# The mixer's head of an S4-plus-MLP block in another order, with its generation phase

## The chip, the cores and the metric
The kernel runs on one core of one Trainium2 chip. The metric is device time in microseconds (us) for one call; the time before is the median of three runs. Profiles come from one execution of each kernel, with a time of its own.

## The reference
One block of width 512 over 2048 tokens, in fp32. A condition vector gives six modulation vectors; the first three belong to a state-space layer (a convolution with a generated kernel, by a Fourier transform), the last three to a mixer (a shift of channels along the tokens, then an MLP of width 1376).

```python
mod = (silu(c) @ w_mod).reshape(1, 6, 1, 512)
sa, ca, ga, sb, cb, gb = (mod[:, i] for i in range(6))
h = layernorm(x) * (1 + ca) + sa
x = x + ga * ssm(h)          # K = Re(sum_n C*dB*exp(dt*A*l)); y = irfft(rfft(h)*rfft(K)) + h*Dskip
h = layernorm(x) * (1 + cb) + sb
g = gelu(layernorm(h) @ w1)  # four quarters of the channels shifted by +1, -1, +2, -2 tokens
x1 = h + shifted(g) @ w2
x = x + gb * (x1 + gelu(layernorm(x1) @ w3) @ w4)
```

## The kernel before
The order of the work is written out by hand; each engine runs its own instructions in program order and waits at each for what it needs. There are five stages.

1. **Preparation** (to about 42 us): angles and weights of the state-space kernel on VectorE and ScalarE.
2. **Generation** (to about 222 us): 32 steps k. `turns(k, 0)` and `turns(k, 1)` build angles on TensorE, and ScalarE takes sine (`sn`) and cosine (`cs`) of them, two steps ahead. `products(k)` on VectorE multiplies them with magnitudes into `e0` and `e1`: the small factor `m1` (line 478), two products with the sine for `e0` (482), one for `e1` (483), one with the cosine for `e0` (484) and one for `e1` (485). `burst(k)` on TensorE sums `e0` and `e1` into the kernel `KX`. Every fourth step `exps` makes the next magnitudes (function Exp, so ScalarE loads another table and then the sine's again). `fill(n)` issues n matmuls whose result nobody reads. The Fourier transform of the input (`u_stats`, `u_norm`, `u_dft`) is spread over these steps.
3. **Spectrum** (to about 354 us): 16 steps multiply spectra; `back` writes `z` through the GpSimd queue to a scratch `ZT` in DRAM.
4. **The mixer's head** (to about 442 us). `load_inv(jh, g)` reads `ZT` back in four blocks for the second half of the channels (jh = 1); `inverse(jh, g)` transforms block g back: token tiles 4g to 4g+3, in two halves i of two tiles each. VectorE adds the result to the residual `X2` (line 692). A mixer group g is two token tiles: statistics of `X2` (`first_stats`), the modulated row `h` (`modulate`: lines 725 and 726), its statistics, on GpSimd the inverse root and the shift (`rs`, `nm`), on ScalarE the normalization (`mix_norm`), on TensorE the transposes `pT`, then the high part `nh` (ScalarE) and the low part `nl` (VectorE, line 751), and two halves of the product with `w1` (`mix_half`: 24 matmuls each, Gelu to `go`, and `mix_out`, which writes `go` to the scratch `GD`). The head works groups 7, 0, 1, 2, 3. The shift is done by reading `GD` with an offset (`chan_load`), so `chan_load(0)` needs the outputs of groups 7, 0 and 1. The weights `w3` and `w4` are loaded (`load_w`) and split in two parts (`split_w`) in between. `chan_w2(0)` multiplies with `w2`, then statistics, `chan_norm(0)`, and the transposes for `chan(0)`.
5. **Channel MLP** (from about 442 us to the end): eight groups `chan(g)`, with the mixer groups 4 to 6 woven into the first of them.

`mix_out` issues from GpSimd's queue; the loads issue from SP's queue. `gop` has two buffers for `go`, `hv` one for `win`.

Of the kernel before, what the change touches and what calls it, by code (L numbers as in the profile page):

```python
# [15 lines left out]
TWO_PI = 6.283185  # L16
# [93 lines left out]
def body(ctx, tc, A):  # L110
# [171 lines left out]
    with tc.manual_schedule():  # L282
# [59 lines left out]
        wr, wi, t0, t1 = tmp("wr"), tmp("wi"), tmp("t0"), tmp("t1")  # L342
        V.tensor_mul(wr, cr, br)
# [26 lines left out]
        V.tensor_mul(mn, mn, mx)  # L370
        at, at0, wn = tmp("at"), tmp("at0"), tmp("wn")
        act(at0, mn, AF.Arctan)
        act(wn, at0, AF.Sin, scale=-1.0, bias=hpi)
        mp = [mod_parts(n) for n in range(2)]
# [11 lines left out]
        V.tensor_scalar(at, at0, INV2PI, None, op0=OP.mult)  # L386
# [13 lines left out]
        V.reciprocal(wn, wn)  # L400
        V.tensor_mul(wn, wn, mc)
        V.tensor_tensor(as4(wn), as4(wn), by(dt), op=OP.mult)
        wps = psu.tile([128, 512], F32, name="pu")
        for i in range(4):
            s = slice(i * 128, (i + 1) * 128)
            T.transpose(wps[:, s], wn[:, s], ident)
        act(WN, wps)
        mod_parts(2)()
        mod_sum(2)()
        load_u(1)  # L410
        V.tensor_mul(mods[1], mods[1], mods[2])
        V.tensor_mul(mods[0], mods[0], mods[2])
# [40 lines left out]
    def turns(k, cos):  # L453
# [10 lines left out]
        o = wk.tile([128, 2, 512], F32, name="cs" if cos else "sn", bufs=3)  # L464
        act(o.rearrange("p a b -> p (a b)"), x, AF.Sin, scale=-TWO_PI, bias=hpi if cos else 0.0)
        return o

    trig = {}

    def products(k):  # L470
        t, u = divmod(k, 4)
        sn, cs = trig.pop(k)
        mg, pt = PE[t][0][u], PE[t][1][:, u]
        e0 = wk.tile([128, 2, 2, 512], F32, name="e0")
        e1 = wk.tile([128, 2, 16, 32], F32, name="e1")
        f2 = lambda z: z.rearrange("p a b -> p (a b)")
        m1 = wk1.tile([128, 16, 32], F32, name="m1")
        V.tensor_mul(m1.rearrange("p d (x y) -> p d x y", x=4),
                     pt[:, :, None, :8].to_broadcast([128, 16, 4, 8]),
                     pt[:, :, 8:12, None].to_broadcast([128, 16, 4, 8]))  # L480
        for a in range(2):
            V.scalar_tensor_tensor(e0[:, 1, a], sn[:, 0], 1.0 - 2.0 * a, mg[:, a], op0=OP.mult, op1=OP.mult)  # L482
        V.tensor_mul(f2(e1[:, 1]), sn[:, 1], f2(m1))
        V.tensor_mul(e0[:, 0], cs[:, 0:1].to_broadcast([128, 2, 512]), mg)  # L484
        V.tensor_mul(f2(e1[:, 0]), cs[:, 1], f2(m1))  # L485
        return e0, e1
# [44 lines left out]
    with tc.manual_schedule():  # L531
        for k in range(2):
            trig[k] = turns(k, 0), turns(k, 1)
        weigh(0)
        for k in range(33):
            now, later = later, []
            if 1 in KP:
                fill(3)
            for f in now:
                f()  # L540
            if k + 2 < 32:
                trig[k + 2] = turns(k + 2, 0), turns(k + 2, 1)
            if k < 32:
# [5 lines left out]
                if fresh:  # L549
                    KP[1] = psk.tile([128, 8, 64], F32, name="kp")  # L550
                    fill(3)
                    for u in range(2, 5):
                        exps(k // 4 + 1, u, u + 1)
                        fill(2)
                if k % 4 == 3 and k < 28:
                    weigh(k // 4 + 1)
            for f in side[k]:
                f()
# [120 lines left out]

    def inverse(jh, g):  # L680
        zz = zis.pop((jh, g))
        for i in range(2):
            p = psy.tile([128, 2, 256], F32, name="py")
            for e in range(2):
                for h in range(2):
                    b = g * 4 + i * 2 + e
                    cc = 15 - b if h == 0 else b
                    T.matmul(p[h * 64:h * 64 + 64, e], FI[:, cc, h], zz[h][:, cc % 4],
                             start=True, stop=True, skip_group_check=True)
            b = g * 4 + i * 2  # L690
            x = X2[:, b:b + 2, jh * 256:jh * 256 + 256]
            V.tensor_add(x, p, x)
# [30 lines left out]

    def modulate(o, b):
        V.scalar_tensor_tensor(o, X2[:, b], mv1[:, b, 0:1], mods[4], op0=OP.subtract, op1=OP.mult)  # L725
        V.scalar_tensor_tensor(o, o, rs1[:, b:b + 1], mods[3], op0=OP.mult, op1=OP.add)  # L726
# [3 lines left out]

    def first_rstd(g):
        rstd(rs1[:, 2 * g:2 * g + 2], mv1[:, 2 * g:2 * g + 2, 1])

    def first_stats(g):
        for b in (2 * g, 2 * g + 1):
            first_stat(b)
        first_rstd(g)
# [18 lines left out]
    def mix_mod_half(g, i):  # L756
        if i == 0:
            mh[g] = (cm.tile([128, 2, 512], F32, name="h2"), cm.tile([128, 2, 2], F32, name="mv"),
                     cm.tile([128, 2], F32, name="rs"), cm.tile([128, 2], F32, name="nm"))
        h, mv, r, nm = mh[g]  # L760
        modulate(h[:, i], 2 * g + i)
        stats(mv[:, i], h[:, i])
        if i == 1:
            rstd(r, mv[:, :, 1])
            P.tensor_tensor(nm, mv[:, :, 0], m_one[:, :2], op=OP.mult)
            P.tensor_tensor(nm, nm, r, op=OP.mult)
            mh[g] = h, r, nm

    def mix_mod(g):
        mix_mod_half(g, 0)  # L770
        mix_mod_half(g, 1)

    def mix_norm(g):
        h, r, nm = mh[g]
# [17 lines left out]
    def mix_out(g, hf, go):  # L792
        P.dma_start(dram(GD, (2 + 2 * g) * 128 + hf * 256 * 2560, [[2560, 128], [128 * 2560, 2], [1, 256]]), go)
# [15 lines left out]
        P.dma_start(dram(GD, (18 if g == 0 else 0) * 128 + hf * 256 * 2560, [[2560, 128], [128 * 2560, 2], [1, 256]]), pd)  # L809
# [102 lines left out]
    def chan(g, hl):  # L912
# [11 lines left out]
        def mod(i):  # L924
            if t is not None:
                mix_mod_half(t, i)
                if i == 1:
# [6 lines left out]
        def half(hf):  # L934
            if t is not None:
                mix_half(t, st["hl"], hf)
                if t < 6:
                    first_stat(2 * t + 2 + hf)
                    if hf == 1:
                        first_rstd(t + 1)  # L940
# [77 lines left out]
    with tc.manual_schedule():  # L1018
# [52 lines left out]
        psw = ctx.enter_context(tp("psw", 2, space=PSUM))  # L1071
        load_inv(1, 3)
# [3 lines left out]
        inverse(1, 3)  # L1076
        load_inv(1, 2)
        first_stats(7)
        mix_mod(7)
        mix_norm(7)  # L1080
        inverse(1, 0)
        hl = parts_of(transposed(mh.pop(7)[0]))
        first_stats(0)
        mix_mod(0)
        first_stats(1)
        mix_norm(0)
        inverse(1, 1)
        mix_mod(1)
        first_stats(2)
        mix_half(7, hl, 0)  # L1090
        nt = transposed(mh.pop(0)[0])
        p1 = mix_w(hl, 1)
        hl = parts_of(nt)
        mix_norm(1)
        go = gop.tile([128, 2, 256], F32, name="go")
        act(go, p1, AF.Gelu_apprx_tanh)
        mix_out(7, 1, go)
        inverse(1, 2)
# [8 lines left out]
        mix_mod(2)  # L1107
        mix_half(0, hl, 0)
        nt = transposed(mh.pop(1)[0])
        p1 = mix_w(hl, 1)  # L1110
        hl = parts_of(nt)
        mix_norm(2)
        go = gop.tile([128, 2, 256], F32, name="go")
        act(go, p1, AF.Gelu_apprx_tanh)
        mix_out(0, 1, go)
        first_stats(3)
        mix_half(1, hl, 0)
        nt = transposed(mh.pop(2)[0])
        p1 = mix_w(hl, 1)
        hl = parts_of(nt)  # L1120
        go = gop.tile([128, 2, 256], F32, name="go")
        act(go, p1, AF.Gelu_apprx_tanh)
# [43 lines left out]
```

## Time and profile before

| | |
|---|---|
| median of 3 runs | 769.93 us (769.35 to 771.09) |
| the profiled execution | 766.72 us, its span 764.9 us |
| TensorE matmul busy | 693.8 us (91%) |
| VectorE busy | 512.9 us (67%) |
| ScalarE busy | 332.8 us (44%) |
| GpSimd busy | 98.1 us (13%) |
| mean granted TensorE clock | 0.952 |

The median lies 3.2 us above the profiled execution. The shares are means over stages that have different limits, so the stages are read one by one: in a stretch where an engine is busy all the time, its work is the limit, and where all of them idle, a chain of waits is. A row of the timeline gives the start, the duration, the engine, the line and the operation; the brackets give the idle time before it and what ended that.

### The profile page before, as it was taken

What the parts mean: (1) busy time and instruction counts of PE and PEld (TensorE: products, weight loads), DVE (VectorE), ACT (ScalarE), POOL (GpSimd) and SP (SyncE); (2) the same over time, 40 slices, a digit from 0 to 9 for tenths busy, and PEclk for the clock granted to TensorE, in tenths of its full rate; (3) what the DMA queues carried; (4) which work ended last, traced back from release to release, by engine and by line L of the source; (5) the groups of instructions that cost most, each with busy time, mean ns of one, the idle gap of its engine ahead of it and who ended that gap; (6) DMA issues with size and microseconds to landing.
All of it is one profiled execution on the core that took longest, in us unless ns stands there. A gap on an engine that the chain in (4) does not pass through costs nothing. (4 is left out here: it accounts for less than half of the span.)

```text
span 764.9 us, 17371 instructions
## 1 busy us (share of the span) xinstructions
PE 693.8 (91%) x7340; PEld 540.2 (71%) x7340; DVE 512.9 (67%) x883; ACT 332.8 (44%) x540; POOL 98.1 (13%) x194
## 2 busy tenths in 40 slices
PE   2799999999989999995578799999999999999993
PEld 1356666665569656662368698999999998998992
DVE  8999999999873576774695696655565545353611
ACT  3678888887843445533133453312223121212120
POOL 1011121110000001000145110112021010100101
PEclk9999999999995899998789799999999999999997
DMA  9523282645259994884316701111110111101001
GB/s 299 164 66 83 71 235 77 168 131 149 57 130 258 243 334 152 274 251 167 137 40 230 246 29 28 29 38 46 32 52 15 42 29 28 28 28 28 9 20 27
DMA packets 51301, 85.51 MB, mean 112 GB/s; under 512 B 5300, under 2 KB 37944, under 8 KB 49560
## 3 DMA queue, kind: packets, MB, share of 16 engines
q1 hardware_dynamic: 44808, 57.92, 27.3%
q0 software_dynamic: 6416, 26.48, 10.5%
q8 instruction: 58, 0.95, 0.5%
q14 instruction: 19, 0.16, 0.1%
HBM read 58.17 MB, written 31.85 MB: 118 GB/s over the span
## 5 line engine op out<-in xcount | busy, mean ns | idle before, releaser
L118 ACT ACTIVATE gh<-pm 128x512 fp32r<-128x512 f32 (+1 forms) x48 | 26.9, 561 | 202.1 <-PE pm L784 202.1
L781 PE MATMUL pm<-nh,w3h 128*128 128x256 f32 (+1 forms) x352 | 87.9, 283 | 0.4 <-ACT nh L118 0.4
L782 PE MATMUL pm<-nh,w3l 128*128 128x256 f32 (+1 forms) x352 | 87.4, 281 | 0.0
L885 DVE TENSOR_TENSOR gl<-gf,gh 128x512 fp32r<-128x512 f32 (+1 forms) x48 | 30.9, 643 | 72.0 <-ACT gf L118 72.0
L894 PE MATMUL pa<-w4h,gh 128*128 128x512 f32 (+1 forms) x176 | 69.5, 395 | 0.0
L895 PE MATMUL pa<-w4l,gh 128*128 128x512 f32 (+1 forms) x176 | 68.9, 391 | 0.0
L781 PEld LDWEIGHTS pm<-nh,w3h 128*128 128x128 f32 (+1 forms) x352 | 65.4, 186 | 2.0 <-ACT nh L118 0.6
L782 PEld LDWEIGHTS pm<-nh,w3l 128*128 128x128 f32 (+1 forms) x352 | 65.6, 186 | 1.7
L784 PE MATMUL pm<-nl,w3h 128*128 128x256 f32 (+1 forms) x352 | 56.1, 282 | 0.0
L784 PEld LDWEIGHTS pm<-nl,w3h 128*128 128x128 f32 (+1 forms) x352 | 47.8, 186 | 0.1
L900 PE MATMUL pa<-w4h,gl 128*128 128x512 f32 (+1 forms) x176 | 47.8, 390 | 0.0
L462 PE MATMUL xx<-MG,ON 64*128 64x512 f32 x160 | 47.4, 391 | 0.0
L463 PE MATMUL xx<-MG,ON 64*128 64x512 f32 x160 | 47.4, 391 | 0.0
L482 DVE SCALAR_TENSOR_TENSOR e<-sn,p 128x512 f32<-128x512 f32 x64 | 41.2, 685 | 4.7 <-ACT sn L118 4.7
L841 DVE TENSOR_TENSOR h<-h,ph 128x512 f32<-128x512 f32 x16 | 11.0, 688 | 45.9 <-PE ph L840 45.9
L502 PEld LDWEIGHTS kp<-e,e 128*32 128x32 f32 x2048 | 30.1, 110 | 14.7 <-issue 9.7
L118 ACT ACTIVATE p<-xx 128x1024 f32<-128x1024 f32 (+1 forms) x40 | 38.2, 983 | 4.3 <-PE xx L254 3.1
L648 DVE TENSOR_TENSOR ma<-pk,us 128x512 f32<-128x512 f32 x32 | 21.9, 686 | 26.0 <-issue 18.2
L484 DVE TENSOR_TENSOR e<-cs,p 128x1024 f32<-128x1024 f32 x32 | 39.0, 1218 | 0.0
L118 ACT ACTIVATE z<-pz 128x512 f32<-128x512 f32 x32 | 17.4, 595 | 49.6 <-issue 33.9
L502 PE MATMUL kp<-e,e 128*32 128x64 f32 x2048 | 35.5, 221 | 2.8 <-DVE e L485 1.9
L900 PEld LDWEIGHTS pa<-w4h,gl 128*128 128x128 f32 (+1 forms) x176 | 33.0, 188 | 6.9
(223 smaller groups left out, 1862.5 us busy)
## 6 DMA issues: line engine op xcount, KB each, us to landing
VU<-vs SPq DMA_DIRECT2D x64, 128.0 KB, 2.6
ld<-VU SPq DMA_DIRECT2D x32, 256.0 KB, 8.2
ZT<-z POOLq DMA_DIRECT2D x16, 512.0 KB, 4.6
ld<-ZT SPq DMA_DIRECT2D x16, 512.0 KB, 5.6
Dw<-in_w POOLq DMA_DIRECT2D x8, 688.0 KB, 4.6
xu<-in_u SPq DMA_DIRECT2D x16, 256.0 KB, 6.7
KX<-in_u SPq DMA_DIRECT2D x16, 256.0 KB, 10.1
GD<-go POOLq DMA_DIRECT2D x16, 256.0 KB, 2.7
```

Source lines behind the costliest of these rows:

```text
L118: return S.activation(out, in_, f, bias=bias, scale=scale)
L462: T.matmul(x[:, :512], la, ma, start=(i == 0), stop=(i == len(ops) - 1))
L463: T.matmul(x[:, 512:], lb, mb, start=(i == 0), stop=(i == len(ops) - 1))
L482: V.scalar_tensor_tensor(e0[:, 1, a], sn[:, 0], 1.0 - 2.0 * a, mg[:, a], op0=OP.mult, op1=OP.mult)
L484: V.tensor_mul(e0[:, 0], cs[:, 0:1].to_broadcast([128, 2, 512]), mg)
L502: T.matmul(kp[32 * j:32 * j + 32, (k % 2) * 4 + g], e1[:, r, d], e0[:, r, :, d * 32:d * 32 + 32], start=(r == 0), stop=(r == 1), skip_grou ...
L781: T.matmul(p, wh[:, k, c], hi[k], start=(k == 0), stop=False)
L782: T.matmul(p, wl[:, k, c], hi[k], start=False, stop=False)
L784: T.matmul(p, wh[:, k, c], lo[k], start=False, stop=(k == 3))
L894: T.matmul(acc[i], gh[:m, e, s], W4h[:m, f], start=(f == 0), stop=False)
L895: T.matmul(acc[i], gh[:m, e, s], W4l[:m, f], start=False, stop=False)
L900: T.matmul(acc[i], gl[:m, e, s], W4h[:m, f], start=False, stop=(f == 10))
```

## The change
All of it moves or merges work; what is computed stays.

- **Preparation.** A scaling of the angle (`at`) moves from VectorE to ScalarE. A reciprocal of a cosine is replaced by a sine, a product and an addition. The transposes of `wn`, the third modulation part and two products of modulation vectors move into the first generation steps.
- **Generation.** Sine and cosine share one tile `tr`, so that the two products for `e1` are one instruction of 1024 columns. `m1` is made for two steps at once. The fills at the top of a step are gone, and those between the exps are fewer (12 to each `exps` before, 5 now). A sine of one column after the exps (`turn1`) brings its table load ahead.
- **Head.** `inverse` is taken apart into halves (`inv_half`) whose matmuls and whose addition stand at different places; two of them use the buffers `pm`. The inverse root of the first statistics is made for each tile. `modulate` is split into `mod1` (line 739) for both tiles of a group and `mod2` (742) later. `keep(n)` issues matmuls that nobody reads, 20 and then 22. Four splits of weights that stood ahead of `mix_half(2, hl, 1)` now stand with the next four, after `chan_norm(0)`.
- **Queues.** `mix_out` issues from SP's queue.

```diff
+        act(at, at0, scale=INV2PI)
         act(wn, at0, AF.Sin, scale=-1.0, bias=hpi)
+        act(ws, at0, AF.Sin)
...
-        V.reciprocal(wn, wn)
         V.tensor_mul(wn, wn, mc)
+        V.tensor_mul(ws, ws, mn)
+        V.tensor_add(wn, wn, ws)
...
-        V.tensor_mul(f2(e1[:, 1]), sn[:, 1], f2(m1))
-        V.tensor_mul(f2(e1[:, 0]), cs[:, 1], f2(m1))
+        V.tensor_mul(e1.rearrange("p r d q -> p r (d q)"), tr[:, :, 1], m1s[0][:, u % 2:u % 2 + 1].to_broadcast([128, 2, 512]))
...
-            if 1 in KP:
-                fill(3)
...
-                        fill(2)
+                        if u < 4:
+                            fill(1)
+                    act(turn1, hpi, AF.Sin)
...
+            if k == 1:
+                V.tensor_mul(mods[1], mods[1], mods[2])
+                V.tensor_mul(mods[0], mods[0], mods[2])
...
+    def mod1(o, b):
+        V.scalar_tensor_tensor(o, X2[:, b], mv1[:, b, 0:1], mods[4], op0=OP.subtract, op1=OP.mult)
+    def mod2(o, b):
+        V.scalar_tensor_tensor(o, o, rs1[:, b:b + 1], mods[3], op0=OP.mult, op1=OP.add)
...
-        P.dma_start(dram(GD, (2 + 2 * g) * 128 + ...
+        Y.dma_start(dram(GD, (2 + 2 * g) * 128 + ...
...
+        def keep(n):
+            d = psT.tile([128, 2, 256], F32, name="pT0").rearrange("p a b -> p (a b)")
+            for _ in range(n):
+                T.matmul(d, W1h[:, 0, :128], W1h[:, 0], start=True, stop=True)
...
-        inverse(1, 3)
+        keep(20)
+        inv_half(1, 3, 1, psy, "py")()
+        first_stats(7)
         load_inv(1, 2)
-        first_stats(7)
-        mix_mod(7)
-        mix_norm(7)
-        inverse(1, 0)
+        a00 = inv_half(1, 0, 0, psy, "py")
+        a30 = inv_half(1, 3, 0, psw, "pm")
+        a01 = inv_half(1, 0, 1, psw, "pm")
+        keep(22)
+        mix_mod1(7)
+        a00()
+        mix_mod2(7, 0)
+        mix_mod2(7, 1)
+        mix_norm(7)
...
-        split_w(4)
+        mix_norm(3)
         mix_half(2, hl, 1)
...
         n = chan_norm(0)
-        split_w(4)
+        split_w(8)
         mix_half(3, hl, 1)
```

How VectorE's rows move in the generation: around one `weigh`, before. `e_1072` and `e_1160` are `e0` of two steps, `e_1073` and `e_1161` their `e1`, `m` is `m1`, `p` the magnitudes.

```order
L478 TENSOR_TENSOR m_1074<-p_545 128x512
L482 SCALAR_TENSOR_TENSOR e_1072<-sn,p_611 128x512 x2
L483 TENSOR_TENSOR e_1073<-sn,m_1074 128x512
L484 TENSOR_TENSOR e_1072<-cs,p_611 128x1024
L485 TENSOR_TENSOR e_1073<-cs,m_1074 128x512
L261 TENSOR_TENSOR p_894<-p_894,WN 128x64x4
L144 BN_STATS lus<-xu 128x6
L145 BN_AGGR lum<-lus 128x2
L478 TENSOR_TENSOR m_1162<-p_894 128x512
L482 SCALAR_TENSOR_TENSOR e_1160<-sn,p_898 128x512 x2
```

The same place now, with `e_1039` and `e_1123` as `e0`, `e_1040` and `e_1124` as `e1`:

```order
L473 SCALAR_TENSOR_TENSOR e_1039<-tr,p_602 128x512 x2
L482 TENSOR_TENSOR e_1039<-tr,p_602 128x1024
L483 TENSOR_TENSOR e_1040<-tr,m_971 128x1024
L261 TENSOR_TENSOR p_873<-p_873,WN 128x64x4
L144 BN_STATS lus<-xu 128x6
L145 BN_AGGR lum<-lus 128x2
L473 SCALAR_TENSOR_TENSOR e_1123<-tr,p_877 128x512 x2
L479 TENSOR_TENSOR m_1127<-p_873 128x1024
L482 TENSOR_TENSOR e_1123<-tr,p_877 128x1024
L483 TENSOR_TENSOR e_1124<-tr,m_1127 128x1024
```

The first step shown makes no `m1` of its own any more, the second makes one of twice the width, and each has one `e1` product in place of two.

VectorE in the head, mixer group 2, before (`h_5201` is its modulated row; the two `nl` rows are the low parts of group 0):

```order
L751 TENSOR_TENSOR nl_5148<-pT_5111,nh_5146 128x512
L751 TENSOR_TENSOR nl_5149<-pT_5112,nh_5147 128x512
L692 TENSOR_TENSOR KX<-py,KX 128x2x256 x2
L725 SCALAR_TENSOR_TENSOR h_5201<-KX,mv_77,modg 128x512
L726 SCALAR_TENSOR_TENSOR h_5201<-h_5201,rs_78,modg 128x512
L721 BN_STATS st<-h_5201 128x6
L722 BN_AGGR mv<-st 128x2
L725 SCALAR_TENSOR_TENSOR h_5201<-KX,mv_77,modg 128x512
L726 SCALAR_TENSOR_TENSOR h_5201<-h_5201,rs_78,modg 128x512
L721 BN_STATS st<-h_5201 128x6
L722 BN_AGGR mv<-st 128x2
```

And now the same group (`h_5166`; the `nl` rows are the low parts of group 1):

```order
L739 SCALAR_TENSOR_TENSOR h_5166<-KX,mv_77,modg 128x512 x2
L768 TENSOR_TENSOR nl_5184<-pT_5172,nh_5182 128x512
L768 TENSOR_TENSOR nl_5185<-pT_5173,nh_5183 128x512
L742 SCALAR_TENSOR_TENSOR h_5166<-h_5166,rs_78,modg 128x512
L735 BN_STATS st<-h_5166 128x6
L736 BN_AGGR mv<-st 128x2
L702 TENSOR_TENSOR KX<-py,KX 128x2x256
L742 SCALAR_TENSOR_TENSOR h_5166<-h_5166,rs_78,modg 128x512
L735 BN_STATS st<-h_5166 128x6
L736 BN_AGGR mv<-st 128x2
L702 TENSOR_TENSOR KX<-py,KX 128x2x256
```

The first multiplications now stand ahead of the low parts, so work that needs neither GpSimd nor ScalarE lies where VectorE may have to wait for `nh` or for `rs`; the additions of the transform back are between the halves.

SP's queue from the last blocks of `ZT` on, before (`ld` the blocks, `w3l` and `w4l` the weights as they are loaded, `win` the shifted window):

```order
L672 DMA ld<-ZT_62 128x4x256 x8
L701 DMA w3l<-Dw_64 128x512 x4
L701 DMA w4l<-Dw_65 128x512 x4
L816 DMA win<-GD 128x256 x4
L701 DMA w3l<-Dw_64 128x512 x4
L701 DMA w4l<-Dw_65 128x512 x4
L701 DMA w3l<-Dw_64 128x352 x4
```

And now:

```order
L807 DMA GD<-go 128x2x256
L823 DMA GD<-win 128x2x256
L807 DMA GD<-go 128x2x256
L823 DMA GD<-win 128x2x256
L715 DMA w3l<-Dw_64 128x512 x4
L715 DMA w4l<-Dw_65 128x512 x4
L807 DMA GD<-go 128x2x256 x2
L830 DMA win<-GD 128x256 x4
L715 DMA w3l<-Dw_64 128x512 x4
L715 DMA w4l<-Dw_65 128x512 x4
```

The outputs of groups 7 and 0 now stand ahead of the first eight weight loads on this queue, those of group 1 behind them, and the window behind those.

206 lines of the change are left out of this document (106 added, 100 removed).

## The prediction
> **What bounds the kernel now.** I read the page first, then busy time by stage, because the shares of the page are means over stages with different limits.
>
> ```profile
> span 764.9 us, 17371 instructions
> 44.00:205.00 161.00, 155.71 (x2478) 97.86 (x2481) 153.74 (x239) 132.84 (x151) 26.02 (x40) 1.00 0.45 121
> 361.00:366.00 5.00, 4.64 (x19) 2.69 (x21) 0.69 (x1) 0.00 (x0) 0.00 (x0) 0.50 1.09 385
> 378.00:407.00 29.00, 23.44 (x170) 20.49 (x169) 26.06 (x50) 10.44 (x16) 12.05 (x29) 0.84 0.28 92
> 407.00:427.00 20.00, 13.05 (x95) 12.00 (x94) 10.27 (x17) 9.47 (x17) 9.19 (x19) 0.86 0.66 219
> 442.00:757.00 315.00, 310.70 (x1976) 281.53 (x1976) 167.03 (x276) 80.25 (x151) 33.95 (x71) 1.00 0.10 29
> ```
>
> The columns are: stretch, its length, busy time (and instructions) of TensorE, its weight loads, VectorE, ScalarE, GpSimd, then the granted clock. From 442 us to the end TensorE has 310.7 of 315 us, so that stage costs what its matmuls cost, and the change leaves them alone. In the generation VectorE has 153.7 of 161 us; TensorE looks as busy, but its row includes fills. In the head nobody is busy: from 407 to 427 VectorE has 10.3 us of 20 and TensorE 13.1. So the time can fall in two places: VectorE's work in the generation, and the waits of the head. Whatever the head saves arrives whole at the end, since only TensorE's fixed work comes after it.
>
> **Generation.** One step of VectorE in the timeline, up to the next instruction:
>
> ```profile
> 143.63 0.69 DVE L478 TENSOR_TENSOR m<-p 128x512 f32<-128x512 f32 x1
> 144.24 1.28 DVE L482 SCALAR_TENSOR_TENSOR e<-sn,p 128x512 f32<-128x512 f32 x2
> 145.45 0.68 DVE L483 TENSOR_TENSOR e<-sn,m 128x512 f32<-128x512 f32 x1
> 146.05 1.22 DVE L484 TENSOR_TENSOR e<-cs,p 128x1024 f32<-128x1024 f32 x1
> 147.18 0.68 DVE L485 TENSOR_TENSOR e<-cs,m 128x512 f32<-128x512 f32 x1
> 147.79 0.74 DVE L429 SCALAR_TENSOR_TENSOR xu<-xu,lum,modu 128x512 f32<-128x512 f32 x1
> ```
>
> By starts, 512 columns take 0.60 us and 1024 columns 1.13. One `e1` of 1024 for two of 512 saves 0.07 us a step. One `m1` of 1024 for two of 512 saves 0.07 in two steps. That is 0.105 us a step, 32 steps: 3.4 us. The two products of modulation vectors (512 columns each, lines 411 and 412) come into step 1; I count one of them, 0.6, as a cost, since the other stands in a wait today, and 2.8 us is left. In the preparation the reciprocal and the scaling leave VectorE, but the first step still waits for sine, cosine and weights from ScalarE, in an order that puts the weights later; I take that at nothing, with one operation (0.7 us) either way.
>
> Merging brings nothing where VectorE waits. How much it waits, and what the fills do to it:
>
> ```profile
> DVE e L482 <- ACT sn L118: 4.7, 4, 2.5
> L491 PE MATMUL kp<-CE,TES 128*128 128x512 f32 x84 | 27.7, 430 | 0.0
> 104.63 1.32 PE L491 MATMUL kp<-CE,TES 128*128 128x512 f32 x5
> 105.89 0.50 PE L462 MATMUL xx<-C,T0S 64*128 64x512 f32 x1
> 103.82 1.82 ACT L118 ACTIVATE p<-xx 128x1024 f32<-128x1024 f32 x2 [0.29 <-PE xx L254]
> 107.17 1.28 ACT L118 ACT_TABLE_LOAD   x1 [1.04 <-PE xx L463]
> 108.46 1.02 ACT L118 ACTIVATE sn<-xx 128x1024 f32<-128x1024 f32 x1
> ```
>
> VectorE waits 4.7 us for the sine, in 4 places. After each of 7 `exps`, five fills stand ahead of the next angles (104.63 to 105.89), ScalarE waits 1.04 us for these, and only then loads the sine's table (1.28). Without those fills and with the table ahead, the sine can start at 107.6, after the table and the eviction that ScalarE has to do anyway: 0.85 earlier. Of the 4.7 us I take 1.7 back (two of the four waits, at 0.85), at least nothing, at most all. Generation: 2.8 + 1.7 = 4.5 us, between 2.1 and 8.2 (2.8 + 4.7 + 0.7). The Trainium skill (ScalarE: Activation LUTs, What ACT_TABLE_LOAD costs) puts a switch at about 2.66 us, load and drain. Here the sine starts 1.29 us after its load, so the trace does not show the drain; by the page, 1.4 us more would be hidden after each of 7 `exps`.
>
> **The head, its front.** The transform back waits for its last blocks.
>
> ```profile
> 362.44 5.74 PE L688 MATMUL py<-ld,FI 128*64 128x256 f32 x30 [0.18 <-DMA ld<-ZT]
> 364.45 0.69 DVE L692 TENSOR_TENSOR KX<-py,KX 128x512 f32<-128x512 f32 x1 [7.76 <-PE py L688]
> 366.15 0.69 DVE L692 TENSOR_TENSOR KX<-py,KX 128x512 f32<-128x512 f32 x1 [1.02 <-PE py L688]
> 418.28 0.18 DVE L722 BATCH_NORM_AGGREGATE mv<-st 128x2 f32<-128x6 f32 x1
> ```
>
> The second block lands at 362.44. VectorE's first addition follows at 364.45 with a clock of 0.50; the statistics of group 7 need the second half, at 366.15. Now the half they need comes first. `keep(20)` fills most of the wait; at full clock the 2.0 us become 1.0, so the first addition comes at 363.45 (at 364.45 if the clock falls anyway). By the Trainium skill (TensorE: Matmul & The Clock Gate, What's actually happening) the clock halves after an idle window of some 3.4 us, and the rest left behind `keep(20)` is shorter; a rule with a shorter window would put the addition back at 364.45, 1.0 us of the sum.
>
> **The head, its body.** The work of VectorE for the five groups, from the groups by line of 354 to 442 us:
>
> ```profile
> L726 DVE SCALAR_TENSOR_TENSOR h<-h,rs,modg 128x512 f32<-128x512 f32 x12 | 9.0, 752 | 3.1 <-POOL rs L717 2.6
> L725 DVE SCALAR_TENSOR_TENSOR h<-KX,mv,modg 128x512 f32<-128x512 f32 x12 | 9.0, 746 | 0.0
> L721 DVE BATCH_NORM_STATS2 st<-h 128x6 f32<-128x512 f32 x12 | 8.3, 692 | 0.3
> L751 DVE TENSOR_TENSOR nl<-pT,nh 128x512 fp32r<-128x512 f32 x11 | 7.2, 682 | 8.4 <-ACT nh L118 8.3
> L721 DVE BATCH_NORM_STATS2 st<-KX 128x6 f32<-128x512 f32 x10 | 6.7, 669 | 0.0
> L692 DVE TENSOR_TENSOR KX<-py,KX 128x512 f32<-128x512 f32 x10 | 6.5, 678 | 8.8 <-PE py L688 8.8
> L722 DVE BATCH_NORM_AGGREGATE mv<-st 128x2 f32<-128x6 f32 x22 | 4.0, 182 | 0.8
> ```
>
> From the first addition to the last statistics of group 3 stand 8 additions (5.4 us), 10 statistics of X2 (6.7), 10 first and 10 second multiplications (7.5 each), 10 statistics of h (6.9), 20 aggregates (3.6) and 8 low parts (5.5): 43.1 us. Today that takes from 364.45 to 418.46, 54.0 us, so 10.9 are waits: for `nh`, for `rs`, and for ScalarE, whose `go` buffers wait for their outputs. The new order puts `mod1`, statistics and additions into just these places, and GpSimd's roots for one tile come while VectorE does the next. TensorE can follow: in 378 to 407 it had 23.4 us of work to VectorE's 26.1. I leave 1.5 us of waits, between none and half of today's (5.5). So the last statistics end at 363.45 + 43.1 + 1.5 = 408.05.
>
> Outputs on SP's queue land no sooner by themselves:
>
> ```profile
> VU<-vs SPq DMA_DIRECT2D x64, 128.0 KB, 2.6
> GD<-go POOLq DMA_DIRECT2D x16, 256.0 KB, 2.7
> ACT go L118 <- DMA GD<-go: 7.0, 4, 3.1
> ```
>
> 2.6 us against 2.7; what goes is GpSimd's time for issuing each, in front of roots. On SP's queue the outputs of group 1 stand behind eight weight loads (2 MB; 5.4 us at the 385 GB/s of 361 to 366), and these are issued ahead of the window's use: I take no loss. In the last stage an output that waits for its `go` has only the next window behind it, which needs it anyway.
>
> **The head, its tail.** Up to the first matmul with w3:
>
> ```profile
> 419.99 1.52 ACT L118 ACTIVATE h<-h,nm,rs 128x512 f32<-128x512 f32 x2 [6.07 <-POOL nm L766]
> 421.89 2.18 ACT L118 ACTIVATE w3h<-w3l 128x512 fp32r<-128x512 f32 x4
> 425.40 1.06 ACT L118 ACTIVATE wh<-win 128x1024 fp32r<-128x1024 f32 x1
> 426.52 0.79 PE L837 MATMUL ph<-w2h,wh 128*128 128x512 f32 x1 [3.20 <-ACT wh L118]
> 430.44 1.69 PE L840 MATMUL ph<-w2h,win 128*128 128x512 f32 x4
> 433.80 1.07 PE L840 MATMUL ph<-w2h,win 128*128 128x512 f32 x4
> 441.85 0.38 PE L781 MATMUL pm<-nh,w3h 128*128 128x256 f32 x1 [0.35 <-ACT nh L118]
> ```
>
> Today: statistics 418.46, normalized 421.51, four splits of w3 (2.18) on ScalarE, `wh` 426.46, two products with w2 (the first cold, 1.69 us for four matmuls that take 1.07 later) to 434.87, first w3 at 441.85. Now from 408.05: +1.53 on GpSimd, +1.52 normalized (411.1), some 1.8 for transposes and `nh` (412.9), `wh` 1.06: 413.95, and TensorE begins. The first product waits for VectorE: two low parts, two multiplications and the split of the window (1024 columns, 1.22 as in line 484), to 416.6, then 1.07: 417.65; the second, warm, takes 2.9 (twelve matmuls at 1.07 to four, less the overlap): 420.55. That is 14.3 us before today's 434.87. But the eight splits now stand together behind the first `go` of group 3: half of its w1 work, which I take to be as long as a product, is 2.9 us, and the eviction 0.55, as one split, so `go` ends near 424.0, eight splits take 4.36 (428.4), the second `go` and one `nh` 1.2. The first w3 matmul starts near 429.6, not at 427.6 where TensorE would be ready. The head's gain is 441.85 - 429.6 = 12.2 us. With the bounds above it is 7.2 (1.0 for a cold clock, 4.0 more waits) to 15.7 (no wait left, and 2.0 from splits that cost nothing).
>
> **Sum.** 4.5 + 12.2 = 16.7 us, between 9.3 and 23.9. Against the profiled execution, span 764.9 and 766.7 us in all, that is 750.0; the median of the runs lies 3.2 us above that execution, at 769.9, and the forecast is set against the median: 753.2 us, between 746.0 and 760.6.
>
> **Rivals.** *The outputs clog SP's queue* (0.12). The window then comes late, or the `go` buffers wait as long as today: for it, the row of 7.0 us, and an in-order queue with 23 weight loads; against it, the slack of the window. It keeps those 7.0 us in the head: 760.2 us.
>
> *The head saves more* (0.08): splits that fit into waits, and a generation that loses all its waits for the sine. That is the upper bound of both, 746, or a few us less.
>
> *The fills were holding the clock* (0.05), slower than before. Without 49 of 84 fills TensorE could fall to 0.50, as it does at 361 us after seven us of idling. TensorE's row has 155.7 us busy in 161, of which 27.7 are fills, so 128 are work. If the share s of that work runs at half clock it takes 128(1+s): it stays below 161 us to s = 0.26, and eats the head's 12.2 us and the saved VectorE time at s = 0.38. At s = 0.5 it is 192 us, 31 too many, and the kernel stands at 769.9 + 31 - 12.2 = 788.7 us. For it: nothing else holds the clock after `exps`. Against it: the 33 us that come free are spread over 28 steps, about 1.2 us each, and the stretch's clock was 1.00.
>
> *The change does not do what it says* (0.03): VectorE's halves only trade places with waits, and the front saves its 1 us alone. Then 769 us, no change that counts.
>
> **Chances.** The forecast has 0.72; the rivals 0.12, 0.08, 0.05 and 0.03. Range: 745 to 762 takes in the bounds and the clogged queue, and leaves out the clock, no change, and a part of the better case, together under 0.2. A difference of 0.2% (1.5 us) is about what a measurement of this kernel can tell. Faster by more: 0.72 + 0.12 + 0.08 + 0.01 of the last = 0.93; within: 0.02; slower: 0.05.
>
> **What would show it.** In the generation, VectorE rows of 1024 columns at 1.13 us from start to start, and the waits for the sine under 4.7 us; its clock at 1.00. At the front, the first addition about 1.0 us after the second block lands. In the body, 43 us of VectorE with under 6 us of waits. In the tail, a wait of TensorE of some 2 us for `nh` ahead of the first w3 matmul. After that 323 us to the end of the span, as today (764.9 - 441.85). I am wrong if the last stage is not those 323 us, if VectorE waits as long in the head as today, or if the clock falls below 1.00 in the generation.

## The result and the profile after

The changed kernel takes 746.30 us (median of 4 runs, 743.56 to 748.32) against 770.51 us before (4 runs beside it, 769.35 to 772.17): the ratio is 0.968, with a 95% interval of 0.9645 to 0.9718. It is faster, as forecast; at 24.2 us the gain is larger than the 16.7 us of the sum, and the time lies inside the range of 745 to 762, near its lower end. The profiled execution after has a span of 744.6 us, 20.3 us below the 764.9 before.

Four rows of each trace cut the program into the same pieces. First the kernel before: VectorE's first and last product of the generation (timeline), the writes of `ZT` by GpSimd (the view of that tile; the last starts at 353.9), and from the prediction the last statistics of group 3 at 418.46 and the first matmul with w3 at 441.85.

```profile
42.76 1.29 DVE L482 SCALAR_TENSOR_TENSOR e<-sn,p 128x512 f32<-128x512 f32 x2
221.78 0.68 DVE L485 TENSOR_TENSOR e<-cs,m 128x512 f32<-128x512 f32 x1
L666 POOL DMA_DIRECT2D ZT<-z x16: 531/531/612, 265.4 to 353.9; - x16
366.88 0.69 DVE L721 BATCH_NORM_STATS2 st<-KX 128x6 f32<-128x512 f32 x1
```

The same rows after, and the first statistics of the head in both (366.88 before, 358.06 after):

```profile
39.21 1.29 DVE L473 SCALAR_TENSOR_TENSOR e<-tr,p 128x512 f32<-128x512 f32 x2 [1.86 <-ACT tr L118]
209.39 1.22 DVE L483 TENSOR_TENSOR e<-tr,m 128x1024 f32<-128x1024 f32 x1
L678 POOL DMA_DIRECT2D ZT<-z x16: 531/531/617, 258.2 to 346.8; - x16
357.33 0.69 DVE L702 TENSOR_TENSOR KX<-py,KX 128x512 f32<-128x512 f32 x1 [7.82 <-PE py L699]
358.06 0.69 DVE L735 BATCH_NORM_STATS2 st<-KX 128x6 f32<-128x512 f32 x1
399.49 0.18 DVE L736 BATCH_NORM_AGGREGATE mv<-st 128x2 f32<-128x6 f32 x1
421.54 0.39 PE L795 MATMUL pm<-nh,w3h 128*128 128x256 f32 x1 [2.11 <-ACT nh L118]
```

| piece | before | after | gain | forecast |
|---|---|---|---|---|
| start to the first product | 42.76 | 39.21 | 3.6 | 0 |
| first to last product (its end) | 179.70 | 171.40 | 8.3 | 4.5 |
| last product to the last write of ZT | 131.4 | 136.2 | -4.8 | 0 |
| write of ZT to first addition | 10.5 | 10.5 | 0 | 1.0 |
| first addition to last statistics of group 3 | 54.0 | 42.3 | 11.7 | 9.4 |
| these to the first matmul with w3 | 23.4 | 21.9 | 1.5 | 1.8 |
| last stage | 323.05 | 323.06 | 0 | 0 |
| sum | | | 20.3 | 16.7 |

The first cut does not stand behind the same work in the two kernels. Before, the first weighting of `p` (line 261), the first `m1` and one of the two products of modulation vectors stand ahead of the first product; in the changed kernel they stand behind it. A row with the same work behind it in both is VectorE's first normalization of the input, at the end of step 1 (line 429 before, 422 after). These rows, and the windows from them to the end of the last product (columns as in the prediction), each of before and of after:

```profile
52.65 0.74 DVE L429 SCALAR_TENSOR_TENSOR xu<-xu,lum,modu 128x512 f32<-128x512 f32 x1
51.01 0.75 DVE L422 SCALAR_TENSOR_TENSOR xu<-xu,lum,modu 128x512 f32<-128x512 f32 x1
52.65:222.46 169.81, 162.82 (x2736) 102.00 (x2736) 161.49 (x248) 139.43 (x159) 23.87 (x36) 1.00 0.42 114
51.01:210.61 159.60, 152.12 (x2697) 94.73 (x2693) 157.29 (x203) 139.93 (x167) 24.50 (x36) 1.00 0.46 121
```

Counted from there, the generation gains 10.2 us (169.81 to 159.60) and all that stands ahead of it 1.6: together the same 11.8. VectorE's work fell by 4.2 us (161.49 to 157.29) and its idling by 6.0 (8.3 to 2.3). Its waits for the sine (4.7 us) and for `p` (0.9) are gone; what is left of waits for the sine after is the one ahead of the first product. By the same row the forecast is 4.9 us for the generation and -0.4 ahead of it, since the product of modulation vectors that was counted as a cost (0.6) and the merging of steps 0 and 1 (0.2) stand ahead of the row.

### The profile page after: what moved, and what is told of

The parts are those of the page before. It is cut to its first block, busy times and chain, and to the rows that moved or that the text cites. A ratio compares the mean times of both kernels' runs of the same rounds, so it can differ in the third digit from the quotient of the medians.

```text
span 744.6 us, 17328 instructions
## 1 busy us (share of the span) xinstructions
PE 690.8 (93%) x7333; PEld 538.7 (72%) x7333; DVE 504.6 (68%) x835; ACT 334.6 (45%) x549; POOL 101.7 (14%) x222
## 4 chain that ended last, share of the span: by engine, by line
PE 47%; DMA 2%; ACT 1%; DVE 1%; issue 1%; SPq 0%; POOL 0%; POOLq 0%; ACTq 0%
PE pm L795 7%; PE pm L798 7%; PE pm L796 7%; PE pa L908 5%; PE pa L909 5%; PE pa L914 5%; PE ph L851 2%; PE ph L852 2%; PE ph L854 2%; PE pT L760 1%; DMA GD<-go 1%; PE py L699 1%; DMA ld<-ZT 1%; DMA w4l<-Dw 1%; DVE st L735 1%
## 5 line engine op out<-in xcount | busy, mean ns | idle before, releaser
L473 DVE SCALAR_TENSOR_TENSOR e<-tr,p 128x512 f32<-128x512 f32 x64 | 41.0, 682 | 1.9 <-ACT tr L118 1.9
L730 POOL TENSOR_TENSOR rs<-mv,eps_t 128x1 f32<-128x1 f32 (+1 forms) x40 | 11.7, 294 | 219.5 <-DVE mv L736 219.3
L660 DVE TENSOR_TENSOR ma<-pk,us 128x512 f32<-128x512 f32 x32 | 21.9, 686 | 26.7 <-issue 17.8
L482 DVE TENSOR_TENSOR e<-tr,p 128x1024 f32<-128x1024 f32 x32 | 39.0, 1218 | 0.0
L483 DVE TENSOR_TENSOR e<-tr,m 128x1024 f32<-128x1024 f32 x32 | 39.0, 1217 | 0.0
```

What stands on the lines that cost most here:

```text
L473: V.scalar_tensor_tensor(e0[:, 1, a], tr[:, 1, 0], 1.0 - 2.0 * a, mg[:, a], op0=OP.mult, op1=OP.mult)
L482: V.tensor_mul(e0[:, 0], tr[:, 0, 0:1].to_broadcast([128, 2, 512]), mg)
L483: V.tensor_mul(e1.rearrange("p r d q -> p r (d q)"), tr[:, :, 1], m1s[0][:, u % 2:u % 2 + 1].to_broadcast([128, 2, 512]))
```

## The experiments

Each kernel was timed beside the kernel before, whose medians in the four comparisons are 769.7 to 770.1 us. "Changed kernel" is the one after.

**Generation alone, head alone.** The edits up to the end of the generation on top of the old head, and the edits of the head on top of the old generation.

> The preparation and the generation of the change alone, the head as before. Theory A (the pieces of the two traces add up: 3.6 us in the preparation and 8.3 in the generation, of which the spectrum stage gives 4.8 back, and the head moves by itself): the last write of ZT lands 7 us earlier and the whole is 7 us shorter, about 763. Rival B (the 4.8 us given back are a hazard of one execution): 12 us shorter, about 758. Rival C (the spectrum stage ends when its transfers end, whatever VectorE does): 770, no change.

> The head of the change alone, preparation and generation as before. Theory A (the pieces add up; from the last write of ZT to the first matmul with w3 the traces show 87.9 us before and 74.7 after): 13.2 us shorter, about 757. Rival B (the head's gain needs the earlier start, because its window and weights are then still on their way): less than 10 us shorter. In both the last stage keeps its 323 us.

Measured: 760.29 us for the first (ratio 0.9894, 0.9858 to 0.9930) and 756.23 for the second (0.9826, 0.9804 to 0.9847). The product of the ratios is 0.9722, just above the interval of the changed kernel (0.9645 to 0.9718); with intervals of their own on both factors (0.9665 to 0.978 for the product, by their ends) nothing speaks against parts that add up. Rival C of the generation and rival B of the head fall; the generation alone gained 9.7 us (5.4 to 10.9 by the interval), between its theory A (7) and its rival B (12). In the trace of the head alone the write of ZT starts at 357.0 and the first w3 matmul at 431.70: 74.7 us, as in the changed kernel (346.8 to 421.54), against 87.9 before. The head's 13.2 us are its own.

The generation's loss behind its last product is mostly one lucky execution of before. With the old generation that piece took 131.4 us in the profile of before, 134.4 in that of the head alone and 133.9 in that of the outputs on SP's queue (below). With the change's generation it took 133.5 to 136.2 in seven profiles (the kernels with an edit in generation work or fills not counted, save `turn1`). The means are 133.2 and 135.1: about 2 us may be given back, and the ranges overlap, so not even that is shown. What tells the executions apart is how long the granted clock (third column from the right) stays at 0.50 behind the last product. The 40 us behind it, before and after:

```profile
222.46:262.46 40.00, 37.71 (x740) 33.95 (x742) 15.17 (x28) 12.95 (x29) 0.00 (x0) 0.66 1.04 250
210.61:250.61 40.00, 37.05 (x664) 34.04 (x666) 11.35 (x19) 11.15 (x23) 0.00 (x0) 0.53 1.05 244
```

That is some 27 us at half clock before and 37 us after. By windows of 4 us it is 27.3 us in the profile of before, 34.1 to 34.2 in the five profiles whose piece took 133.5 to 134.5 us, and 37.3 to 37.6 in the four whose piece took 135.8 to 136.2.

The preparation has such a case too. The row behind equal work came at 52.65 to 52.77 us in three profiles with the old preparation; with the change's it came at 51.01 in the profile after and at 52.15 to 52.99 in the other six. So the usual gain there is 0.2 us, not 1.6. The profile after is the only one of all whose clock is 1.00 from 30 to 40 us; each of the others has a stretch at half clock there. The profile after, and that of the next experiment:

```profile
30.00:40.00 10.00, 7.55 (x38) 4.26 (x42) 7.24 (x12) 6.57 (x10) 0.00 (x0) 1.00 0.75 203
30.00:40.00 10.00, 7.74 (x28) 4.62 (x30) 8.51 (x9) 5.03 (x8) 0.00 (x0) 0.83 0.77 209
```

From the row to the last product the stretch is steady: 169.7 to 169.9 us in the three, 159.6 in all seven. With these, the pieces sum to 0.2 + 10.2 - 1.9 + 13.2 = 21.7 us, at the lower edge of the interval of the whole (21.7 to 27.4 us).

**Reciprocal back on VectorE.**

```diff
-        act(ws, at0, AF.Sin)
...
+        V.reciprocal(wn, wn)
         V.tensor_mul(wn, wn, mc)
-        V.tensor_mul(ws, ws, mn)
-        V.tensor_add(wn, wn, ws)
```

> The changed kernel with the weights made by a reciprocal on VectorE again (3.35 us) in place of a second sine on ScalarE and two operations of VectorE (in all 2.0 us more on VectorE). Theory A (the reciprocal itself stood on the path to the first step): the first product of the generation comes 2 us later, and the whole takes up to 2 us more, 748. Rival B (it was the order, weights behind the first sine: the first product waits 1.9 us for the sine in any case): the first product comes within 0.3 us of the changed kernel's 39.2, and the whole is at 746 to 747.

Measured: 745.20 us (0.9702, 0.9651 to 0.9754). The first product comes at 40.46, which misses the 39.2 of rival B; but that 39.2 is the execution at full clock, and in the nine other kernels without the reciprocal the first product comes at 40.34 to 41.10. In mechanism rival B holds: the reciprocal lies in the wait for the first sine, which is 1.05 us here and 1.85 to 3.26 in those nine. The row behind equal work comes at 52.26, as in the others. The first product stands earlier than before because the weights now come behind it, and they cost there what they cost ahead of it.

**The old fills.** The fill(3) at the top of a step and two fills after each exps again, without `turn1`; then, as a kernel of its own, only `turn1` removed.

```diff
+            if 1 in KP:
+                fill(3)
...
-                        if u < 4:
-                            fill(1)
-                    act(turn1, hpi, AF.Sin)
+                        fill(2)
```

> The changed kernel with the old fills of TensorE in the generation (three at each step, two after each exps) and without the early switch to the sine (turn1). Theory A (the fills ahead of the angles and the late table made VectorE's 5.6 us of waits: 4.7 for the sine, 0.9 for p): these waits come back, first to last product of the generation takes 175 to 177 us instead of 171.4, and the whole 750 to 752. Rival B (the waits went with the new order of angles and the fused operations): 171 to 172 us there, and the whole at 746.

> The changed kernel without turn1, the small sine after each exps that brings the sine's table early; the fills stay as in the change. With the old fills and without turn1 together, the generation took 184.0 us instead of 171.4. Theory A (it was the fills: with them fewer, the angles are ready when ScalarE is, and the table of 1.28 us is loaded while VectorE still has work): first to last product 171.4 to 173 us, the whole 745 to 748. Rival B (it was the table: 1.28 us more ahead of the first sine at each of 7 exps, and VectorE has no slack there): 175 to 180 us, the whole 750 to 755.

Measured: 756.43 us (0.9827, 0.9801 to 0.9853) with the old fills, and first to last product 183.99 us; 746.62 (0.9702, 0.9673 to 0.9732) without `turn1`, and 171.40 us. VectorE's waits in the generation (engine, what waited, for whom: us in all, times, longest) are, with the old fills:

```profile
DVE e L472 <- ACT tr L118: 9.7, 7, 3.1
DVE e L481 <- ACT tr L118: 1.2, 1, 1.2
DVE p L261 <- ACT p L118: 0.8, 1, 0.8
```

So the fills did it, and the early table nothing. One mechanism showed in a size nobody expected: I had put the waits at 4 to 6 us, and they are 11.7. With VectorE's steps shorter, the fills that TensorE still has to do ahead of the next angles push every sine after an exps past the point at which VectorE needs it. The switch of the table, by ScalarE's timeline with the old fills and then without `turn1` (the first row lists its wait as issue, so it names no releaser; the same row of before, in the prediction, names TensorE's angles):

```profile
109.76 1.28 ACT L118 ACT_TABLE_LOAD   x1 [1.02 <-issue]
111.05 1.02 ACT L118 ACTIVATE tr<-xx 128x1024 f32<-128x1024 f32 x1
104.15 1.28 ACT L118 ACT_TABLE_LOAD   x1
105.45 1.03 ACT L118 ACTIVATE tr<-xx 128x1024 f32<-128x1024 f32 x1
```

Without the fills the load follows ScalarE's last eviction with next to no wait. The sine that it leads to starts at 105.45, against 105.29 with `turn1` in the kernel with the reciprocal back, whose first product comes at the same time (40.47 and 40.46): `turn1` only lets the load and that eviction change places, and VectorE does not wait for either.

**The merged operations taken apart.** `m1` for each step and `e1` as two operations of 512 columns.

```diff
-        V.tensor_mul(e1.rearrange("p r d q -> p r (d q)"), tr[:, :, 1], m1s[0][...])
+        for r in range(2):
+            V.tensor_mul(e1[:, r].rearrange("p d q -> p (d q)"), tr[:, r, 1], m1)
```

> The changed kernel with e1 and m1 as operations of 512 columns again, the rest of the change kept. Theory A (an operation costs about 0.07 us beside its columns, so 32 + 16 operations more cost 0.07 times 48, 3.4 us): first to last product takes 174.8 us instead of 171.4, with no wait for the sine, and the whole 749.7. Rival B (VectorE was waiting anyway, the longer work only fills waits): below 172.4, and the whole within 1 us of 746.

Measured: 751.23 us (0.9771, 0.9735 to 0.9807), first to last product 178.99 us, 7.6 more than in the changed kernel. In that execution one wait of 4.0 us stands among them; the other 3.6 are the 3.4 of theory A. From the row behind equal work on, VectorE's work is 160.41 us against 157.29, 3.1 more, where the 30 steps behind it should give 3.15. The whole is 1.5 us above theory A's 749.7. The wait of 4.0 us is the rival that the prediction gave 0.05, in small (windows, then VectorE's row, then the wait's):

```profile
140.00:144.00 4.00, 3.23 (x46) 1.67 (x46) 4.00 (x7) 3.86 (x4) 0.99 (x2) 1.00 1.05 243
144.00:158.00 14.00, 14.00 (x132) 7.86 (x125) 10.41 (x17) 9.45 (x12) 1.97 (x3) 0.51 0.45 124
158.55 1.29 DVE L473 SCALAR_TENSOR_TENSOR e<-tr,p 128x512 f32<-128x512 f32 x2 [3.99 <-PE kp L500]
```

In 140 to 144 TensorE has gaps and matmuls of 32 rows; at 144 its clock falls to 0.50, and for 14 us it is the limit, until VectorE waits for `kp`. Of the nine other profiles with 35 fills one (`warm_gap`, below) shows such dips too, at 44 to 52 and at 104 to 108 us, with 1.2 us of waits; the other eight show 1.00 from 44 to 205 us. That fewer fills are behind it is not shown: the kernel with the old 84 dips at 44 to 52 us too.

**Outputs back on GpSimd; outputs on SP's queue alone.** One word in two lines of `mix_out`, in the changed kernel and, the other way, in the kernel before.

```diff
-        Y.dma_start(dram(GD, (2 + 2 * g) * 128 + ...), go)
+        P.dma_start(dram(GD, (2 + 2 * g) * 128 + ...), go)
```

> The changed kernel with the outputs of the mixer issued by GpSimd again instead of on SP's queue. Theory A (GpSimd's 0.75 us for each issue and the wait of the go buffers stood in the chain of the head): 4 to 7 us slower than the changed kernel, 750 to 753, with ScalarE's waits for GD<-go back in the head. Rival B (the order of the head alone removed those waits): within 1 us of the changed kernel, 746.

> The kernel before with one edit: the outputs of the mixer are issued on SP's queue instead of by GpSimd. The changed kernel with its outputs back on GpSimd lost 6 us. Theory A (queue and order add up: the queue alone is worth 6): 764, with ScalarE's wait for GD<-go (7.0 us before) mostly gone. Rival B (in the old order the outputs of group 1 stand on SP's queue behind eight weight loads, and the waits for nh and for the roots stay): 768 to 772.

Measured: 752.36 us (0.9766, 0.9738 to 0.9794) with the change's order and GpSimd's queue, 6.1 above the changed kernel (by the trace 4.9 of it between the first addition and the last statistics of group 3); 768.81 (0.9992, 0.9975 to 1.0009) with the old order and SP's queue, no difference. The waits in the head, two rows of the first and two of the second:

```profile
ACT go L118 <- DMA GD<-go: 3.5, 1, 3.5
DVE nl L768 <- ACT nh L118: 8.0, 4, 2.9
ACT go L118 <- DMA GD<-go: 4.2, 1, 4.2
DVE nl L751 <- ACT nh L118: 9.7, 3, 6.0
```

The queue is worth 6 us in the new order and nothing in the old one, where a `go` still waits 4.2 us for an output that stands behind the weight loads, and the wait for `nh` grows from 8.3 us to 9.7. In the changed kernel `go` has no wait for its outputs, and `nl` waits 4.8 us.

**Without the idle matmuls of the head.** Both `keep` calls removed.

> The changed kernel without the idle matmuls of the head (keep(20) and keep(22)). Theory A (the trace after shows the clock at 0.50 in 354.3 to 357.3 in spite of keep(20), so that one does nothing; keep(22) covers 5 us in which TensorE would be idle ahead of the transposes): the first statistics are as late after the write of ZT as in the changed kernel (11.3 us), and the whole is 0 to 1.5 us slower. Rival B (the prediction's step: keep(20) holds the clock and is worth 1.0 us): the first statistics come 1.0 us later after the write of ZT.

Measured: 744.85 us (0.9676, 0.9648 to 0.9703), no difference from the changed kernel that counts; the first statistics 11.5 us after the write of ZT starts, against 11.3. What goes on in the changed kernel at that place (windows; the clock is the third column from the right, ahead of DMA share and GB/s):

```profile
352.00:354.00 2.00, 0.00 (x0) 0.00 (x0) 0.00 (x0) 0.00 (x0) 0.00 (x0) 1.00 1.02 345
354.00:357.00 3.00, 2.62 (x9) 1.22 (x10) 0.00 (x0) 0.00 (x0) 0.00 (x0) 0.54 1.09 385
```

`keep(20)` ends at 352.0, the blocks land from 354.1 on, and 2.1 us of idling are enough for the clock to fall just when the matmuls come.

**The clock behind the generation.** 15 fills around the last burst (`warm_gap`); and with two dense matmuls more in each round of `k_first` (`warm_all`).

```diff
+                if k == 31:
+                    KP[1] = psk.tile([128, 8, 64], F32, name="kp")
+                    fill(8)
                 burst(k, *e)
+                if k == 31:
+                    fill(7)
```

> The changed kernel with 15 fills around the last burst of the generation, and two dense matmuls (128 rows, 128 columns) more in each of the eight rounds of k_first, whose clock is 0.50 in the traces before and after. Theory A (the clock falls in the 2 to 3 us of idling ahead of k_first, and its matmuls of 32 rows never bring it back): the rounds take 2.1 to 2.9 us instead of 3.41, and the write of ZT comes 4 to 10 us earlier: 736 to 742. Rival B (the stage behind ends with its transfers, whose queues are full from 210 to 280 us): shorter rounds, but ZT within 1 us of now, 746. Rival C (the clock is lowered by something else than idling): rounds of 3.4 us or more, and 746 to 749.

> The changed kernel with the 15 fills around the last burst of the generation alone; k_first as in the changed kernel. Theory A (the clock falls by the idling ahead of k_first, not by its matmuls): the rounds take 2.1 us until something stalls TensorE, ZT is written 4 to 10 us earlier after the last product, and the whole takes 736 to 742. Rival B (matmuls of 32 rows let the clock fall by themselves, as in the kernel before, where it went to 0.50 in the first round): one or two rounds of 2.1 us and then 3.41 again, 744 to 746.

Measured: 745.00 us (0.9682, 0.9662 to 0.9702) with the fills alone, 751.63 (0.9765, 0.9735 to 0.9795) with the dense matmuls too. In the first, the eight rounds of `k_first`, by VectorE's copies, begin like this, and the windows behind show the clock:

```profile
218.74 0.69 DVE L611 COPY VK<-pk 128x512 f32<-128x512 f32 x1 [2.80 <-PE py L607]
220.52 0.69 DVE L611 COPY VK<-pk 128x512 f32<-128x512 f32 x1 [0.50 <-PE py L607]
222.31 0.69 DVE L611 COPY VK<-pk 128x512 f32<-128x512 f32 x1 [0.50 <-PE pz L607]
216.00:222.00 6.00, 5.94 (x193) 5.52 (x191) 2.58 (x4) 2.17 (x4) 0.00 (x0) 1.00 1.00 294
222.00:226.00 4.00, 2.21 (x46) 2.07 (x43) 1.38 (x2) 1.09 (x2) 0.00 (x0) 0.69 1.01 267
226.00:244.00 18.00, 15.98 (x293) 15.61 (x290) 5.35 (x8) 4.35 (x9) 0.00 (x0) 0.50 1.08 246
PE py L607 <- issue: 3.8, 3, 1.8
```

Rounds take 1.79 us at full clock instead of 3.4, until TensorE issues nothing for 1.8 us, with no releaser in the trace; within that stall the clock falls to 0.50 (between 223.5 and 224.0), and it does not come back in `k_first`, although TensorE is busy nearly all the time. In the other kernel four rounds stayed at 1.00, a stall of 2.0 us followed, and the rounds behind it, with their dense matmuls at half clock, took 5.3 us. So the matmuls of 32 rows did not bring the clock down by themselves in these two executions: 5.5 us of them went by at 1.00 in the first. That speaks for theory A on the cause, though the 745.00 us are the time of rival B. On the gain theory A is wrong: the last write of `ZT` comes 133.0 us behind the last product, against 133.5 to 136.2 in the seven profiles above (141.4 with the dense matmuls), since the stall ends the warm rounds after three or four of eight, and the generation of `warm_gap` took 1.8 us longer in that execution.

**Both waits of the head mended.** keep(32) for keep(20), and four of the eight splits ahead of `chan_w2(0)`.

```diff
-        keep(20)
+        keep(32)
...
+        split_w(4)
         chan_w2(0)
...
-        split_w(8)
+        split_w(4)
```

> The changed kernel with keep(32) in place of keep(20), so that TensorE idles less than 1 us ahead of the last blocks, and with the first four of the eight splits of w3 and w4 moved ahead of the products with w2, where ScalarE has 10 us with no work. Theory A (the front loses its time to the clock, which falls 2.3 us after keep(20) ends, and the tail to the splits ahead of nh): the first statistics come 1 us earlier after the write of ZT (10.2 instead of 11.3 us), the first matmul with w3 1.5 to 2 us earlier after the last statistics of group 3 (20 instead of 21.9), and the whole takes 743 to 744. Rival B (the blocks themselves end the wait at the front, and VectorE's four subtractions delay the products with w2 by what is saved): no part moves by over 0.3 us, 746.

Measured: 743.25 us (0.9663, 0.9647 to 0.9678). By the trace, theory A holds in both parts: the clock stays at 1.00 through the matmuls on the last blocks, the first statistics come 10.4 us after the write of ZT instead of 11.3, and the first w3 matmul 20.2 us after the last statistics of group 3 instead of 21.9.

```profile
352.00:357.00 5.00, 5.00 (x22) 3.57 (x20) 0.00 (x0) 0.00 (x0) 0.00 (x0) 1.00 0.82 251
357.00:360.00 3.00, 1.93 (x11) 0.86 (x12) 1.78 (x4) 0.00 (x0) 0.13 (x1) 1.00 1.09 384
PE pm L795 <- ACT nh L118: 0.3, 1, 0.3
```

TensorE's wait for `nh` ahead of w3 fell from 2.11 us to 0.3. This is the best version of the study: faster than before, and 3 us below the changed kernel by the medians, where the intervals of the two still overlap.

## Why the prediction was right, and where its sizes were off

- **Where the time falls: right.** VectorE's generation and the waits of the head gave it, and the last stage took 323.06 us, as the 323.05 before.
- **Merging: right.** Taken apart, it costs 3.6 us against the 3.4 of the sum (3.1 against 3.15 behind the row of equal work). VectorE's work fell by 4.2 us there; what the other 1.1 are, no run separates.
- **The waits for the sine: mis-sized, and half of the reason wrong.** The step "two of the four waits, at 0.85" put 1.7 us. All of them went, and 0.9 for `p` that the step had not counted: 5.6 us, more than the upper end of 4.7. The fills are the cause, as argued; the table ahead of the sine is worth nothing. With the Trainium skill (ScalarE: Activation LUTs, What ACT_TABLE_LOAD costs) a switch would hide 1.4 us more of drain behind its load; here the sine starts 1.30 us after the load of 1.28 starts, so no run shows that drain.
- **The preparation at nothing: right.** The step saw that the first product waits for sine, cosine and weights, and that the weights now come later. By the row behind equal work the gain is 0.2 us in most executions, within the 0.7 either way; the 1.6 of the profile after go with its clock. The reciprocal, 3.35 us of VectorE's work, lay in a wait.
- **The front: right sum of small things, wrong cause.** `keep(20)` was to hold the clock and bring the first addition 1.0 us closer to the write of ZT; it came no closer (10.5 us in both). The statistics came 1.7 us closer, since the half that they need is first. The prediction named its condition: a rule with an idle window shorter than the 3.4 us of the Trainium skill (TensorE: Matmul & The Clock Gate, What's actually happening) would put the addition back. 2.1 us of idling did; the measurement decides against that window as a safe margin. The trace of before had shown it: the prediction read the clock at 361 us, after seven us of idling, but it was down much earlier. TensorE's last matmul ends there at 354.39, and the clock is:

```profile
355.00:356.00 1.00, 0.00 (x0) 0.00 (x0) 1.00 (x2) 0.00 (x0) 0.00 (x0) 1.00 1.01 418
356.50:357.00 0.50, 0.00 (x0) 0.00 (x0) 0.19 (x1) 0.00 (x0) 0.00 (x0) 0.50 0.00 0
```

- **The body: nearly right.** 44.6 us forecast, 42.3 measured. The waits left are 1.9 us (0.25 and 1.66 for `nh`) against 1.5; the work was put too high, since neighbouring instructions overlap by some 0.1 us and the sum of durations counts that twice.
- **The tail: right, with its wait.** 21.6 us forecast, 21.9 measured; the eight splits kept TensorE waiting 2.11 us for `nh`, where the text said some 2.
- **The clogged queue: did not happen, but the queue counts.** No wait for an output is left. The sum gave the queue no term of its own; it is worth 6 us of the head's 13.2, in the new order only.
- **The clock in the generation: did not happen in the changed kernel**, at 1.00 in 44 to 205 us; in two other kernels with the same fills it did, for 4.0 us and 1.2 us of VectorE's waits.
- **The better case: half of it came.** The rival with a chance of 0.08 put 746 us, and 746.30 were measured. Its generation that loses all waits for the sine is what happened; its splits that cost nothing are not, by TensorE's 2.11 us.
- **The distance in all.** The generation (10.2 us against 4.9; of the difference 3.9 are the waits for the sine and `p`, 5.6 against 1.7), the head (13.2 against 12.2) and the preparation with steps 0 and 1 (0.2 against -0.4) make 6.9 of the 7.5 us between the forecast gain of 16.7 and the measured 24.2. The two traces differ by 20.3 only, since the profile of before was a favourable execution: its piece behind the generation took 131.4 us, against 133.9 and 134.4 in the other two with that generation. The prediction had set its sum against the median, where this does not enter.

## What to carry to other kernels

Matmuls that only hold the clock stand in TensorE's queue like all others: ahead of work that another engine waits for they cost more the faster that engine gets (the waits in the generation were 5.6 us before and 11.7 with the merged operations), so count them on the path before trusting them. When two edits share a chain (an order of work and the queue that its outputs take), try each alone: here the queue was worth 0 us without the order and 6 us with it. Cut two traces only at rows that have the same work behind them: here the first product had moved ahead of other work, and the preparation seemed to gain what the generation did. And compare the profile's own execution with the medians stage by stage, before a difference of two traces is read as a gain or a loss.

## What the runs showed of the hardware

The granted clock fell after 2.1 us without matmuls in the changed kernel (352.0 to 354.1) and before (354.39 to 356.5), after 4.2 us without the `keep` calls (346.75 to 350.9), within a stall of 1.8 us (`warm_gap`), and in `unmerged` at 144 us behind 4 us with gaps of at most 0.45 us among matmuls of 32 rows. Behind the generation the time at half clock came in three sizes, 27.3, 34.1 to 34.2 and 37.3 to 37.6 us: about 3.4 us apart, once and twice. At half clock, 20 us and more of `k_first`, with matmuls of 32 rows and 64 columns and TensorE busy nearly all the time, did not bring it back, in the kernel before too:

```profile
230.00:254.00 24.00, 23.54 (x400) 22.28 (x398) 9.02 (x14) 7.86 (x15) 0.00 (x0) 0.50 1.07 250
```

At full clock a round costs 1.79 us and at half clock 3.4; eight rounds would be 13 us shorter, an estimate of the most that a warm `k_first` could give, and no run shows it. In nearly all profiles TensorE had stalls there that no engine released (0.2 to 3.8 us in sum, listed as issue), in stretches with a DMA share of about 1.0. What is behind these stalls no run separated.
